# A new order of steps for a gated attention with an MLP behind it, on one core

## The chip, the core and the metric

One core of a Trainium2 chip runs the whole kernel as one program. The metric is the device time of an execution in microseconds (us). The engines are named as in the profile: PE (TensorE), DVE (VectorE), ACT (ScalarE), POOL (GpSimd) and SP (SyncE, which issues all DMAs here). Each engine runs its instructions in the order in which the program lists them; between engines, semaphores keep the data right.

## The reference, cut to what matters

```
# gateloop: B, H, S, D = 4, 8, 768, 48
mag = sqrt(a_re*a_re + a_im*a_im)
scale = minimum(mag, 0.999) / (mag + 1e-6)
a_re_n, a_im_n = a_re*scale, a_im*scale
for t in range(S):
    new_re = ar*S_re - ai*S_im        # ar, ai: row t of a_re_n, a_im_n
    new_im = ar*S_im + ai*S_re
    kv = outer(k[t], v[t])            # for each batch and head
    S_re, S_im = new_re + kv, new_im
    y[t] = q[t] @ S_re
# act_prelu: 3072 tokens, d_model 384, d_ff 2048
x = y.transpose(0, 2, 1, 3).reshape(B*S, H*D)
h = x @ w_in
g = maximum(h, 0) + alpha * minimum(h, 0)
out = g @ w_out
```

All of it is float32. A state of 48 x 48 complex numbers runs through 768 tokens for each of 32 heads, with a complex gate for each token and row; its outputs are the tokens of a two-layer MLP with a PReLU.

## The kernel before, in words

The scan over tokens is done in chunks of 128 tokens: 4 batches of 6 chunks make 24 units, each for all 8 heads. Within a unit the gate's magnitude and phase are applied by a tree of levels 1, 2, 4, 8, 16 and 32.

The work is written as 39 generators, the tasks. Each `yield` ends a step, and a step issues one instruction or a few. A task's letter is its place in the list.

- **Gates, letters A to I** (`gates`, from line 223). Gate A makes the decays and phases of the first chunk of batch 0, B those of chunks 1 and 2, C those of 3 to 5; D to I take three chunks of a batch each. The large steps are DVE's (the products L338, the sums L340, the last products L426 and L429) and ACT's (the functions L257 to L281, the copies L366 and L368 that turn a pair of re and im into three). In gates with 3 chunks, the small products of the phase scan are cut: the level of 128x72 (L338) and its sum of 128x36 (L340) run on GpSimd for the late gates, seven of each, then come ACT's copies L366 and L368, a second short chain on GpSimd (128x12 and 128x6), again L366 and L368, and further steps with L391, L396, L405, L407 and L413. The results go to DRAM (decs, phs).
- **Loads, letters J (q, k, phases PP and decays T of each unit), K (half rows of v, copied from DRAM to DRAM, L560), L (v in several row orders, L603 to L629), M (the raw weights, L491)**, and **n** (the MLP's input xT, L873).
- **Weights, letters N and O.** Each weight piece comes as 64-bit words and is made into float32 by three ACT steps (L507, L509, L511), one on GpSimd (L515, 128x768) and two on DVE (L517, L519).
- **Units, letters P to Z and a to m** (`unit`, from line 645). A unit turns keys and queries by the phase (DVE, L661 and L663), multiplies them up the levels (DVE, L717, six times), has copies of half of them made (ACT, L740 and L756), multiplies keys with queries on PE (L678) and masks the results (L699 on ACT, L702 on DVE). Then come transposes (PE, L785), the state's update (PE L797, DVE L826 and L829), the outputs (PE L817 and L841), their copy from PSUM (ACT, L855) and a DMA to DRAM (ysc).
- **The MLP, letter o** (`all_mlp`, line 926). The 24 units' tokens make 14 groups: two of one unit, ten of two units, two of one. For each group and each of 16 blocks of 128 features: three matmuls (L889) into ps_h, ACT's Relu (L896), DVE's scaled sum (L898). With a block of lag come the output matmuls (L908) into ps_o; after 16 blocks ACT copies ps_o out (L918) and SP sends it (L921). ps_h has two buffers, ps_o one.

Buffers come from pools: three KQ, one PP, two T, one V and one VL, two xT, three states St, two ps_lv, one tile for each of ps_misc and ps_y.

What sets the order of all work is one string, ORDER (from line 30), with one letter for each step: `Plan.run` (L96) goes through the string and advances the task of each letter by one step. The numbers that the steps yield (estimated durations and what they wait for) are not used when the kernel is built. So an engine's queue is exactly the order in which the string reaches its instructions, and a buffer is reused in the order in which the string reaches its tiles. The string has 4292 letters. GpSimd is told from DVE in the gates by the size of the step (`small`, `on`), not by the string.

```
    def run(self, order):
        for c in order:
            next(self.tasks[self.LETTERS.index(c)], None)
```

Of the kernel before, what the change touches and what calls it, by code (L numbers as in the profile page):

```python
# [27 lines left out]


ORDER = (  # L30
    "AABAMMAAAAAAAAAAAAAAAAAMAAAAAMABJMNAJNNABNAAAAAAAAAAAAANKJKAKBKNBAABAAAABABBJAAAALAAAAAAABAMAAAAOKAK"
# [4 lines left out]
    "ooCRCNCRLRMKOCCOCDONCJDQQMNDQCODNCRDCDRCCQNQOLCQCROCOMLRCLRMOCLODoDQJCLCCRQKRCCQCooLooLCLRQDLLLLLLCN"
    "QoRCDRDCDCoCKCCRCRCCCoRRRDoCKRRooRQCRCoCoooCJQQQRQooDRNoDoRRRQDJCRDRoNooooJooJoooRJoDoooORDooooooLLL"
    "LLLoooDODoDnoRDooRoOoERDRooNNRRLDoRoSRRoooNOoNooSoEooOoooNOSLOoSoNROSSoooSJDooSJJSJSLSJOooooooSSSooS"
    "SLSoDooELoLLSSooooooDSSLESoJSJoSSSSSooDooSSToDoooSDoSoETDEDTDoJoSSoSSJJSSEDoTSoooKJoTTooKooLDDoEoDoS"
    "LTKTToToDoDLSoLoDoTKoEEDTDSSoTTToSDDDLDoJLSoSSSooooSoDoDDEoooDToTToooDoEoLoooLDTnooDUoDLooEooooooEDo"  # L40
    "oEToTTDDDDDToToDJJJETJUooDoTDToooUoTTLLLEooLooooLToDUDETUTUUToETTTToUoDLDDoUDUDoUDTDoooooUooKDoKTLUo"
    "EUTUTTTEDDDLDoEEEoDoooooJJoDoTTKKoTToooELoooEDoooooTLUUDUULoLooLooLLoooooDoUDEUooEoETEoDooDoooooEooo"
    "LooLUUUUoEUUEoUEoLEEoooooUEUoEoUooEEooEUoooJoVUUUUJJUoJUEUVUUEoUUUUEEVJEEEFVoVooVoJoooooVVVoJUVUoooV"
    "oJFEoVVoJonoJooVWooVooWVVFoEFVLoooLoVEoLLLLLLVoooWLooooVoLWEEEEEEEEEEEEEEEoLooLoLoLKWoWVFJVEEVWJVVVo"
    "VooWooVVVoooVoWoVoKWWVoVJVVWoVVWWJEVVFEEEEEVEEJEEEWWVoLWooWoLoLLLLLEWLoEEXoFEKoLooEoWWWEFWXVWWFLWVEo"
    "LLVFLLooWVoooVVVVFJJJJEJoooWoooWEooWEWooWWWWEWEEWWEWWWEooWEWoLEXLWFoWFLoooLoXoLWoWoLoLoEoFooXXFXooFX"
    "oooooFELWLoLJXLJLoKoXXooLooFoooFoXoooooXXXFFXoooXXoXoooFFooFFXXoXLXXYooXFXFooXWJFXoXJooXnoXXYoYoooXX"
    "XooJJJoYFoFXFFoGXFXXFJLXXFYYFXFFXYXLXLXooGoLLLFXoooXooLJXooYoYLYFFoJJoooYoooGFoKYoFoFoooJYFFFYYZFGFo"
    "ZFFoFoYooJooYoYoooYooGooZoZFYYYYFYoFFFFYFJFJFFLoFooLoYoooYoJoLYYLooGoYLZLZYoooYoGYYYYFYFLZFLLZZGYFYY"
    "LFoYFZYYGYFLZFFFFFFZGFFFFFFaoYYoFoYoooooYYLLoZZZoLZoZnoLoZoooooooJFFLoLLLLZGJJJoJFoZFFFFZoKZGoZZFaFZ"  # L50
    "FooooooZZFZoKZoooFFooFooooZZooZZZZZZFZJZoZZGGZoZoZFooaZZZZooaGGaLoZGLoaaGJooLoooaaoLLLLaLJooJaJoLoaG"
    "ooooooLooooooaaooGabaooGooboooooaoGaboaLoHGHoGboooobGooboooGaaabaaaaGaabooKKGJoGaLLbbKoaoooaGGbboGoo"
    "GaoaaaaJaGaGoaKGaaHHaGaGaJGoGGGGoaGoJoaooaoKKooHoHHLooGcGoGoJbbGoGoocHoooooooLbboLLLGGGboJJJJobcoLoo"
    "oGooLoLGLocbbobooGGoooooocbcLLLbbbbbcnoboboHbGJcboobcoocooLLbbooobbcHGGbbbcbHoGoGGGGcLcGcGbGHLLLLobH"
    "HbGJHLLLGocobboobGLGGcGGGoccboooboooGoLGLGooHGoocccoGHocLdbdbbcocGoccGoJcGGooLLoocooHcGoHooGGoJKcGoJ"
    "JGGGGGGGHoooooocodcccccoHLLLLoLLoooLdooLoccGGGoHdoodooodLHdoIdoooooodJodoIoooooooLLLHHcocooooodLHooo"
    "oHooddccdooododHHdcodoJIoHHcHdddddddddHHHcoocoooKJccoHLooooooooodoooeJdHooJooondooddHHdHdHdJedoJdIdo"
    "dJddIddddoHooeoHodoJdHoooLedJJJeIeeeHeHoHooLeHoooLHIeooooooHJHeoooeLILeLHoLoLeooLIoLeeJfefofKooofHeo"
    "oooooLoooLoefefeofLeoooeIJeIILoeeooeoeHHHeHHHoHHHHHHHofeoJoIeoeeefeoefeeeIIefeeIJeooeoooIofeeooIeooo"
    "eoLLfffIfooHooooJofffIoIoooJLgJoggHLJHHHHHooooLLooooKHLoLoHoJLoLKLKLLLHgHHfggooIHHfooonffffoffHoooJf"  # L60
    "foHHofooKHHfoKfggHggoooIIIIoHooHoffffHfffffffHooLLHLHHLoLoooooHoHoIogHoooHoooIoIofHgooooooIoofIoIfLo"
    "HIIfLLLLLggggKoIoooooogJgooooIfoKgoooooLoggfgoLoohggIhggoooghogoIgoooJggoIohJooIJgggggggggJKgIIggJJI"
    "ghooIhLggoohohoLoogLJLohhoJhhooohhooooJooohhhioohIIoJoihoooIIooIihooiohnoooooooLIIILLohihihLhoohhhJo"
    "IhhoooLoohiJLLoLoLIIoiIIhIIIohIhILIioooIhhhhhhhhhLhJhoohIIIiiiIJIooLIIIoIhIIIIhhoojLhLooohooooooiiio"
    "iojLiooooJiJioJLLLojoIjoLoooLLLLLoooooooiIiIJIiijiIjiiiIooooIiiIoiooIjioIoooooIojIIIooIooooJioiiIjii"
    "ijoiiLiiLiLILiiiojoijooiIioLjiLjJIjILIoLoLojoooJoJjoooojoooooooJoooojoojjJojoojJoLooLoooookLoooojLko"
    "ookLojjjjokojoJkknJoJoookoojoookjoooojoooojjkkjjlojjokLkkkkjLLLLLLLLjLokooooookoookkoooooojokkkkkkkj"
    "okjjjjjoooLLooooLLooookkoooooooooooooojoookooookokokkkkkkkkokkkjJloooooooooooooooookJoolookookolooll"
    "llolLoookooolJloJJoJkoolLoJoomlkllolnooooooooloooooooJJmlooLooooolmooooooomooolmolmooollolllLLoooooL"
    "moLoLLooloomolmlLLmLLoolooooloLlmooooooooooolllllmmLoommmLooooooooooooooooooooLoooooooommooooomLoomm"  # L70
# [930 lines left out]
```

## Time and profile before

| what | value |
|---|---|
| median of 3 runs | 836.58 us (833.38 to 837.02) |
| profiled execution | 836.36 us |
| its span in the trace | 834.6 us |
| mean granted TensorE clock | 0.962 |
| PE busy | 695.8 us, 83% of the span |
| DVE busy | 651.7 us, 78% |
| ACT busy | 438.7 us, 53% |
| GpSimd busy | 200.6 us, 24% |
| DMA | 130.91 MB, 157 GB/s on average |

The span runs from the first to the last instruction in the trace; the execution's own time is 1.8 us longer. Busy time counts compute instructions only. In the rows of instructions, a name such as "ps_h<-xT,w_in_sb" gives the output and the inputs, then the shape (partitions x elements), then how often. A wait is written as the engine that idles, the line that it then runs, and what released it.

### The profile page before, as it was taken

Reading aid. Unit: us, or ns where it says so; the run is one execution under the profiler, and the core shown is the slowest. Engines: PE = TensorE matmul, PEld = TensorE weight load, DVE = VectorE, ACT = ScalarE, POOL = GpSimd, SP = SyncE. Lnnn points to the kernel's source line nnn. Section 1 sums busy time; section 2 is a strip of 40 time slices with the busy share of each in tenths; the row PEclk is TensorE's granted clock in tenths of the full one; section 3 lists DMA queues with packets and bytes.
Section 4 is the critical chain, followed back from the end, with each engine's and each line's share of the span. In section 5 each row is a group of like instructions: output and inputs, shape, how many; then the busy total and the mean of one; then the engine's idle time right before and its main releaser. Section 6 shows DMA issues by size and latency. Waiting matters only on the chain.

```text
span 834.6 us, 26848 instructions
## 1 busy us (share of the span) xinstructions
PE 695.8 (83%) x11488; PEld 527.7 (63%) x11488; DVE 651.7 (78%) x1020; ACT 438.7 (53%) x937; POOL 200.6 (24%) x293
## 2 busy tenths in 40 slices
PE   0001435889998999899999999999999999999998
PEld 0001424667776777677777777777777777777776
DVE  5989999999997899889988988979767652644112
ACT  7758787467635665565657446644344342323221
POOL 5231222328603600360135103330341000000000
PEclk9999755899999999999999999999999999999999
DMA  6696977786478579737873586457834832511110
GB/s 195 189 280 157 274 170 227 217 220 175 100 222 209 145 171 248 186 88 197 233 194 77 158 259 159 115 143 216 210 99 118 202 70 61 136 34 43 35 30 10
DMA packets 194174, 130.91 MB, mean 157 GB/s; under 512 B 74120, under 2 KB 185864, under 8 KB 194056
## 3 DMA queue, kind: packets, MB, share of 16 engines
q1 hardware_dynamic: 194056, 129.20, 58.8%
q8 instruction: 90, 1.47, 0.7%
q14 instruction: 28, 0.23, 0.1%
HBM read 100.82 MB, written 35.71 MB: 164 GB/s over the span
## 4 chain that ended last, share of the span: by engine, by line
PE 53%; DVE 23%; DMA 12%; POOL 4%; issue 4%; ACT 4%; SPq 1%; DVEq 0%; ACTq 0%; POOLq 0%
PE ps_o L908 22%; PE ps_h L889 20%; DVE KQ L717 4%; DMA T<-decs 4%; PE ps_lv L678 4%; DVE gate L426 3%; DVE gate L338 2%; PE ps_y L817 2%; DMA phs<-gate 2%; PE ps_y L841 2%; PE ps_kv L797 2%; DVE gate L429 2%; DMA g_sb<-in_w_out_dram 1%; POOL gate L338 1%; DVE gate L340 1%
## 5 line engine op out<-in xcount | busy, mean ns | idle before, releaser
L889 PE MATMUL ps_h<-xT,w_in_sb 128*128 128x256 f32 (+1 forms) x1344 | 297.3, 355 | 9.0 <-DMA xT<-ysc 7.0
L908 PE MATMUL ps_o<-w_out_sb,g_sb 128*128 128x384 f32 x768 | 297.2, 500 | 7.9 <-DVE g_sb L898 4.5
L889 PEld LDWEIGHTS ps_h<-xT,w_in_sb 128*128 128x128 f32 x1344 | 235.7, 194 | 82.1 <-DMA xT<-ysc 7.8
L898 DVE SCALAR_TENSOR_TENSOR g_sb<-g_sb,al,ps_h 128x256 f32<-128x256 f32 (+1 forms) x224 | 97.5, 436 | 117.9 <-ACT g_sb L896 117.6
L896 ACT ACTIVATE g_sb<-ps_h 128x256 f32<-128x256 f32 (+1 forms) x224 | 78.8, 352 | 200.7 <-PE ps_h L889 199.4
L908 PEld LDWEIGHTS ps_o<-w_out_sb,g_sb 128*128 128x128 f32 x768 | 136.5, 191 | 59.4 <-DVE g_sb L898 7.0
L717 DVE TENSOR_TENSOR KQ<-KQ,T 96x1024 f32<-96x1024 f32 x120 | 149.2, 1246 | 23.8 <-PE ps_lv L678 15.2
L678 PE MATMUL ps_lv<-WQ 96*32 96x32 f32 x2304 | 34.3, 204 | 72.6 <-DVE WQ L661 56.2
L678 PEld LDWEIGHTS ps_lv<-WQ 96*32 96x32 f32 x2304 | 26.5, 116 | 92.7 <-DVE WQ L661 56.2
L740 ACT COPY WQ<-KQ 96x1024 f32<-96x1024 f32 x48 | 49.9, 1040 | 22.2 <-DVE KQ L717 22.2
L338 POOL TENSOR_TENSOR gate<-gate 128x72 f32<-128x72 f32 x42 | 25.8, 615 | 134.3 <-ACT gate L368 131.5
L515 POOL TENSOR_SCALAR top<-top 128x768 f32<-128x768 f32 x16 | 41.2, 2578 | 65.2 <-ACT top L507 65.1
L756 ACT COPY W<-KQ 96x512 f32<-96x512 f32 x48 | 30.9, 644 | 40.1 <-DVE KQ L717 30.3
L338 DVE TENSOR_TENSOR gate<-gate 128x576 f32<-128x576 f32 (+5 forms) x84 | 48.6, 579 | 3.8 <-ACT gate L368 2.4
L855 ACT COPY T<-ps_y 48x256 f32<-48x256 f32 x96 | 31.6, 365 | 34.5 <-PE ps_y L841 33.7
L817 PE MATMUL ps_y<-A,VL 64*48 64x64 f32 x2304 | 42.0, 224 | 4.4 <-issue 3.8
L426 DVE TENSOR_TENSOR gate<-gate 128x1152 f32<-128x1152 f32 (+2 forms) x36 | 43.6, 1235 | 0.1
L817 PEld LDWEIGHTS ps_y<-A,VL 64*48 64x48 f32 x2304 | 39.7, 125 | 5.4 <-issue 4.5
L699 ACT ACTIVATE A<-ps_lv,columns 128x64 f32<-128x64 f32 x144 | 37.6, 334 | 9.2 <-PE ps_lv L678 9.1
L678 PE MATMUL ps_lv<-KQ,W 96*32 96x32 f32 x1536 | 24.5, 203 | 20.3 <-ACT W L756 19.7
L702 DVE TENSOR_TENSOR A<-ps_lv,mask 128x256 f32<-128x256 f32 x96 | 37.6, 412 | 0.0
L717 DVE TENSOR_TENSOR KQ<-WQ,T 96x1024 f32<-96x1024 f32 x24 | 29.5, 1231 | 6.4 <-DMA T<-decs 4.2
(106 smaller groups left out, 899.4 us busy)
## 6 DMA issues: line engine op xcount, KB each, us to landing
T<-decs SPq DMA_DIRECT2D x48, 384.0 KB
PP<-phs SPq DMA_DIRECT2D x24, 387.0 KB
KQ<-in_q_dram SPq DMA_DIRECT2D x48, 192.0 KB
decs<-gate SPq DMA_DIRECT2D x7, 1152.0 KB
phs<-gate SPq DMA_DIRECT2D x14, 576.0 KB
KQ<-in_k_dram SPq DMA_DIRECT2D x40, 192.0 KB
vsc<-in_v_dram SPq DMA_DIRECT2D x48, 144.0 KB
VL<-vsc SPq DMA_DIRECT2D x24, 288.0 KB
```

Of the source, the lines that this page charges most:

```text
L338: on(4 * k).tensor_tensor(out=m, in0=w[:, 1::-1].unsqueeze(2).to_broadcast([P, 2, 2, k]), in1=pairs_of(u), op=ALU.mult)
L426: TT(out=m[:, a], in0=U5[:, 1 + a], in1=turned(off3, o)[:, a].unsqueeze(1).unsqueeze(3).to_broadcast([P, L // 2, nb, 2]), op=ALU.mult)
L515: nc.gpsimd.tensor_scalar(out=top, in0=top, scalar1=F64_SMALL, scalar2=None, op0=ALU.max)
L678: nc.tensor.matmul(t[64 * i + j:64 * i + j + HC // 2, p], lhsT=keys(n, g), rhs=queries(n, g), start=True, stop=True)
L699: nc.scalar.activation(a[:, :, cols], t[:, :, at:at + name], AF.Copy, scale=s)
L717: nc.vector.tensor_tensor(out=x, in0=x if x0 is None else x0, in1=m, op=ALU.mult)
L740: nc.scalar.copy(z.rearrange("p i n t -> p i (n t)").rearrange("p i (m h) -> p m i h", h=h), bass.AP(tensor=KQ.tensor, offset=KQ.offset + ...
L817: nc.tensor.matmul(o, lhsT=Vp[h][64 * i:64 * i + 64, s, e_ * D:(e_ + 1) * D], rhs=a, start=False, stop=False)
L889: nc.tensor.matmul(p, lhsT=w_in_sb[:, f // 2, kk, f % 2 * P:(f % 2 + 1) * P], rhs=x_of[m][:, kk], start=(kk == 0), stop=(kk == NK - 1))
L896: nc.scalar.activation(gt, p, AF.Relu, scale=-1.0)
L898: nc.vector.scalar_tensor_tensor(out=gt, in0=gt, scalar=al_1[:, f:f + 1], in1=p, op0=ALU.mult, op1=ALU.add)
L908: nc.tensor.matmul(sums[0], lhsT=gt[:, c * P:(c + 1) * P], rhs=w_out_sb[:, f], start=(f == 0), stop=(f == NF - 1))
```

## The change

The string ORDER is another one. Nothing else differs: the same 4292 letters, each as often as before, the same functions, buffers and instructions on each engine. Since the order inside a task is fixed, only the way in which the tasks are woven into each other differs. The new string was chosen by a search that counts the holds of GpSimd and VectorE on each other and the length of the DMA queue. Of the diff, which replaces all 43 lines, the first two lines and the last two:

```diff
 ORDER = (
-    "AABAMMAAAAAAAAAAAAAAAAAMAAAAAMABJMNAJNNABNAAAAAAAAAAAAANKJKAKBKNBAABAAAABABBJAAAALAAAAAAABAMAAAAOKAK"
-    "AOBAAABMAAABAAABBBABLLBABAOMABAKBABABBBALNBNABABAABBOBAKBNBABBNOBNBOOOABBBOBMBBBNLONNBBBBBBOBLBBBOBN"
...
-    "ooooooooooooooooooooomoooooooooooooooomooommmmmmmmmmmmmoooooooooooommnoooooooooooooooooooooooooooooo"
-    "oooooooooooooooooooooooooooooooooooooooooooooooooooooooooooooooooooooooooooooooooooooooooooo"
+    "AAABAAAAAMAAAAAAAAAAAAAAAAAMMMBAAAAMJNAAAAAAAANJNNAAABANANAABBAABAJAKJABAAMAAAABBAAAAAABAOAAOAAKABAA"
+    "LMAAABAAABABBBLBALBABOAOMBAABLBBBNABAABABNAABABBNBABALABLOBOMBNBBKKONOBOBBNBBBJLBOBJBOBLBNBBBJBBBBBB"
...
+    "oooooooooooooooooooooooooooommmmmmmmmmmmmmmoooooooooooooooooooonoooooooooooooooooooooooooooooooooooo"
+    "oooooooooooooooooooooooooooooooooooooooooooooooooooooooooooooooooooooooooooooooooooooooooooo"
 )
```

Placed instruction by instruction, the two orders differ as follows (work of the same engine that stands ahead of it, each piece at its duration in the trace of before). The mean shift is 1.3 us on PE, 1.4 on DVE, 1.2 on ACT and 0.2 on GpSimd. Larger moves are these:

- Ahead of the first feature matmuls of the first group stand 100.7 us of DVE work, before 90.3; ahead of the second group's 166.9 in both.
- The half-row copies K stand eight places earlier among SP's DMAs, on average; the weight loads M stand a few places later, the one of 126.27 us two places.
- In the head, unit 2's copy L740 and gate C's second L368 stand behind the ACT step L507 of the weight piece that this load feeds.
- ACT's steps of gates G, H and I (L366, L368 and the steps behind them) stand earlier by up to 21 us of ACT's time. The memset of gate I (L305) stands behind gate H's first chain on GpSimd, where it stood within the gate's chains.

More of the change, by code (lines that the diff above doesn't have):

```diff
@@ L30 @@
 ORDER = (
-    "AABAMMAAAAAAAAAAAAAAAAAMAAAAAMABJMNAJNNABNAAAAAAAAAAAAANKJKAKBKNBAABAAAABABBJAAAALAAAAAAABAMAAAAOKAK"
-    "AOBAAABMAAABAAABBBABLLBABAOMABAKBABABBBALNBNABABAABBOBAKBNBABBNOBNBOOOABBBOBMBBBNLONNBBBBBBOBLBBBOBN"
-    "NOBBJBKJBNJBPBBBBBOBPBBPBBBPBCCBBOBKBPPPBNLBMPJCKBBCPLBLKKPBMBBOPKKOKBBCBPBCBPMBCBPBLPBNCLPLCPLBPBCP"
-    "CLPCCCNPJJJCJONJNPCDCPPPPPPPPPPDPCPPCJMPCCPKPCPCQCQCNOCDPJCNCQCNLQCCPQJJCPCPQCDQPPNOPOCOQCOPJPCQPPPC"
-    "DOQMCQNCQDLJQJnCQLQJCQCKKKLQDDQKOLCCKoQCKNONCQLLNCRCQNQCRQCQRNQDQQKCQMQODLCLRDQCRLNRRDDCLLORCQOLCQON"
@@ L36 @@
[L36 to L70, printed above, removed]
@@ L71 @@
-    "lllllomLlLlllooloooooooooLLLoomlooLlnommooooooooooommLomooomooooooooooooooooooooooooLLmooooooooooooo"
-    "ooooooooooooooooooooomoooooooooooooooomooommmmmmmmmmmmmoooooooooooommnoooooooooooooooooooooooooooooo"
+    "AAABAAAAAMAAAAAAAAAAAAAAAAAMMMBAAAAMJNAAAAAAAANJNNAAABANANAABBAABAJAKJABAAMAAAABBAAAAAABAOAAOAAKABAA"
+    "LMAAABAAABABBBLBALBABOAOMBAABLBBBNABAABABNAABABBNBABALABLOBOMBNBBKKONOBOBBNBBBJLBOBJBOBLBNBBBJBBBBBB"
+    "NBBNBBBKOBBPBPBPBBBBOPOLBNPBBCJBPCLOMBBCMNBKKBPKKKKBBPPBPMKCBPBBBOKOBCPBBBPPCBLBBJPPLPBNPKCCJCBCPCCC"
@@ new lines @@
+    "JNNPCPCPBPCOLCPPPPPPPKNPCKPKNLJCPPJJPCDNPPKCPJCCCNDCPPOJKKCQPCNNPCPPOLJLNOCLCCMOMQCPQQCOQCQQCQCQCDPL"
+    "PDQPPPQCDDQQQCLQPNJCCOCQCOQCQCCQCNDCJLRCQQKQCCLnNJCRJLCDDDQQOCORNCCQNQQLOOQQCLKCOKCKRDCoDJNLDRNQCCNC"
+    "MDLJLLCNCRMQDQCORQCQQORMCNKRCRoNODDCDOCNRQRCOQCOCCCCCQKOCMJQOLLoCRQLORCDCLLRKoDRQDLLLCCQNooooCQRRLCR"
+    "QQDQCCoDJLLDoCCoCDCMoooRoDQoRCQLLLoRoDRRDCCCoooRoQDDCCRRDoNRRODRNRoooRRDooDnRRoRRoooooDOoLLJoRNOoJDo"
+    "oooJDLooooRooLNooNoDRooOJRODROSSooRNoLooooooOooSooENooRSooRSoSJSNoRSERRLRSoSSooooOJLLSJLoooDoSooESJL"
@@ new lines @@
+    "LSoSSOoSSoJoLoooooEoLSLDSSDooooSoSSSTSJoSSDoooTSSSooDEToooDSESSSJDoSSooToooSooETJTSJLTLooTTDLoDDDDDE"
+    "KSoooJToESSDoDTDoEToLoSKSoSDDoKSTTToooDoDoooJooDKEDSSoooDTTTDoLooTooLooooEooToEEJoEooUoTooUDEoooDooT"
+    "DoDDoLTooJTLLLLLLTDooULooooTETTooTooDToEoDUDDDDDDDDTUoUooTTUoEooUnoUKDUDUKKoooToJJJDJEoETTTTLLLoUoDU"
+    "DULEEoELoTUooTLKDoUDoELLoKDoTDDooDoDDDoooDEDTToEooLLoEooDoooUoooooTToTooDUooLDoEoTEoUooDooooUUEoooTo"
+    "EoEoUoLUUooUUTEoUEEooULEoooUooUoEUKoJJEooEoooUEUJoJUUUUUoVUEUVJUUVFVVEooEUUUVooooooJoVJVEUUoEVFoEVEE"
@@ new lines @@
+    "JooVnVJoJooLVooooooFoWooooWVoVoFFVEEEELLLLLLVLLLooVVWooVooooooEVEEoEooWooWooVVVWoLLWWWEEEEEELEEVVVVV"
+    "ooEoVooVLooFVWVEooVVJVJFJVJKVWEFVVWWWEoVJEEEEEVooWFLXLLLEEWEEooWooLoLooooLWEVVWEVEWEKWXEVVVVWLLLLWLo"
+    "WFoooEWEEEELEoWoVVooWWEEooooLWEFFWooooooWoEJFoJoWooWWWJEEEEWoWWLoXLoLoEFFooooWoWooooJLLWXXXWFWWWoLXL"
+    "ooLoXXWWLoJXWFooWoooXoJooFXoooFXXoXoXooXXJooXoLooFoooFoXXXXLoLYLXXoXLXJoonoXXoXoXooXJXoJJFGFYXFoXoYY"
+    "FoFooGGoXXXFFXFKoKFKYFXYFFYFXFFooFFJYoLoooooLYoXoYXXXoJoFooLoFYFJFFGoLLLLoooooXoXXXYYoYoYYoYooYJJFoY"
@@ new lines @@
+    "oooooJooZoYYFFYYoZYGYoYoFoLFooooZoLoZooooJoFZZYLZYFoYoFFooJYFFFFFFFFFFFFFFFYoYLLLLoKGZGYYYYYJYZYKJoY"
+    "YLLZYYGoLZGoooKoLoZYYKooLFFFGLZLLLGZYYFYZYZoFoFFFFFFFFoFKZZoZFFooFooaoFoFoooaooZGoZFLLLZLLFJZoFZFZJZ"
+    "FZooZoFooZZGFFFoFFoonoooFooooGZoZooZaZFZoJZZoJooGoZZoJooZZaoooaaaGaZZZoZZJZLGJZZoaooLLLGoooooaGaoJoo"
+    "oLbooKooJooooLGooabGaGbaoaGaoooGoaaoooooaoGoooLLGLooboobooboaabababaGaooaJoLLaaLoaoaooaaoGJLJGGGGoGo"
+    "HGaaaHaaaoGJaaoabGGGGJbGLbGLaaLGHoLaaLooLaobcHGoaoooJJbooJoooGooHGbbooLGoHoobbobobcoooGGHbooGcoooooo"
@@ new lines @@
+    "oGGGGGGoHooooobbcbHbccbLLcGLLobHLbLooboGKGboGGGGobooobocbbLGcHcoocGoKbcGGJGGGGbbbHbbbKGbcbJGJccGGGcn"
+    "LooJLLLGLGLLLcHLLLLLcHooLcoooGobbbcGcbbGGbbccooobGGooGooodoJJooocoHcGcHHGoocodooooooKGoooccJGGHoGooo"
+    "oGooGcooococHGoJoHooGcccGdccoJcGcLGooodHHHLoHLooooJKoooLHddodHoHodododGodoooLLoooIcooodIoocdodHLdodc"
+    "HcdLcoHdooccLLHLdIJoHHHcHooHoooocoLoodIdoddoKoodocddddoooeooddooLooodoHHooHooHKHoooLoodHoHodJdHHHHoH"
+    "HHIJJdddddJedHoHndddHHdJJLdHeooJooLedodooeddeeoeoLooLHeeeIooHoooooHHHHHHHHHHooHKeoeJJeLoIIeooooofoLo"
@@ new lines @@
+    "LeLLLfeLLoooooeefIfooooooooeefeeeooefefoeeoHHHHHeeofIHoooHLLoeHfIooHHHooHeHeeeeIHeeeeeefJeHfoHJIoHeL"
+    "oefHoJIoHLoJIffoffeJeIIeeLoofoJoooofHLLooofoogIoooffJfoofffoHofofofLooJLLLogofooJKLIofooHLoHogooongo"
+    "HLLfoLgKHgHgooooooooooooofogogJIfgfffffIgIfffHLJIIoogfIIfILHKoHofHfooLLooooooggLgffgoooooogooooggoIo"
+    "ooIHffgILIgogIgIogoLoILIoggooIgoJoLoooLoooILILIIoooogogooghIoLgohoggghhgJogJgggJggooKJgJJggIoIooghhJ"
+    "gIIIIohoohgoooohoooooIIIIihIJIoIIIoIJoIooioIoohoJLhhJoooooooooLohLhIihIIIIIhiLoLLLLLLLLLLoonohoooooo"
@@ new lines @@
+    "hhoooohiohoihoohIIIIIoooihhhiohoJhJohiIhiioohooooIIIIIIIIIohoohhhhhhioooooooohhohooiohihhIIIooooiihh"
+    "IiohhiooooooLoihohiJiiiLJLJLoLLLooooiLLLjLiooIIoiiJjooIojjIIioIIooooooooLojjjLIooooooiooioJoLoijoioo"
+    "iiIijJiiijJLoIjiiiiiiiiiioIoooooooIiIoLoooInjLLoojjooooooLjjoooojoooJoojjoooJJooLjjjjjjjkkojooojoooo"
+    "oooLkoLokLjoooojookkkkkoLLjooLLoLkookojokojjjjjkoJkkokLLokoooojjkJJJoooLooLoooookjookjkkjkokLjkoojoo"
+    "kjojkoLokkooLoooooLooooLoooLoooojJolLLkjlLoookkoLokkkjkJkJkkkkkkoookooJlJoooooooookoLookolkJLklJJoko"
@@ L73 @@
+    "loooooloooonJooooJomoloolololoooooooooooooLoooooollllomolomloloooooloooooooooooLommlmLlLLooloooooooo"
+    "ooooollolloommmmoLoloollooooooolmloLLLLLLoomlommmmllolllooolmommololmlmmlomlllloommLLLLLLmooLooooooo"
+    "oomooolollooooooooooooooooooooooooooLooooooommmLLoLonooooooooooomLLmoooooooooooooooooooooooooooooooo"
+    "oooooooooooooooooooooooooooommmmmmmmmmmmmmmoooooooooooooooooooonoooooooooooooooooooooooooooooooooooo"
     "oooooooooooooooooooooooooooooooooooooooooooooooooooooooooooooooooooooooooooooooooooooooooooo")
```

## The prediction

> **What bounds the kernel now.** The page comes first, with the slices of PE and DVE (busy tenths, 40 slices).
>
> ```profile
> PE   0001435889998999899999999999999999999998
> ...
> DVE  5989999999997899889988988979767652644112
> ```
>
> A slice is 20.9 us. PE is full only from the ninth slice on, and DVE is full from the second to about the twelfth. So the kernel has a head, in which VectorE sets the pace, and a body, in which TensorE does. The view of busy time by stretches puts numbers on both. Its columns are us; PE, PEld, DVE, ACT and POOL busy (and instructions); granted clock, DMA share, GB/s.
>
> ```profile
> 0.00:60.00 60.00, 0.66 (x32) 0.52 (x32) 46.59 (x138) 39.34 (x62) 24.60 (x38) 1.00 0.79 218
> 60.00:100.00 40.00, 12.47 (x428) 10.70 (x428) 39.79 (x55) 33.05 (x47) 7.43 (x4) 0.95 0.80 216
> 100.00:160.00 60.00, 30.61 (x742) 25.21 (x743) 58.17 (x101) 42.88 (x74) 17.15 (x9) 0.58 0.73 198
> 160.00:184.00 24.00, 19.68 (x306) 15.15 (x305) 23.92 (x42) 15.12 (x29) 6.37 (x4) 0.93 0.94 253
> 184.00:400.00 216.00, 203.40 (x3675) 154.37 (x3674) 196.44 (x268) 124.56 (x281) 77.24 (x119) 0.99 0.68 174
> 400.00:560.00 160.00, 159.25 (x2732) 119.60 (x2731) 141.72 (x197) 94.53 (x202) 48.20 (x84) 1.00 0.65 169
> 560.00:834.60 274.60, 269.74 (x3580) 202.13 (x3578) 145.08 (x225) 89.27 (x246) 19.64 (x35) 1.00 0.37 97
> ```
>
> At 184 us the second group of feature matmuls starts (L889). Up to there DVE is busy 46.59 + 39.79 + 58.17 + 23.92 = 168.5 us, so it idles 15.5, most of it in the first stretch; PE is busy 63.4 of the 184. After 184 PE is busy 632.4 of 650.6 us. The span is then the time at which the head lets PE go (184), plus 632 us of matmuls that no order can shorten, plus what PE still idles, 18.2 us. What the change could win in the body is a part of these 18; what it could win in the head is DVE's idle time and whatever lengthens DVE's instructions. PE's own list of waits, from 184 us on, says what the 18 are made of (us in total, times, longest).
>
> ```profile
> PE ps_o L908 <- issue: 3.0, 1, 3.0
> PE ps_y L841 <- DVE St L829: 2.2, 2, 1.5
> PE ps_h L889 <- DMA xT<-ysc: 2.1, 1, 2.1
> PE ps_lv L678 <- ACT W L756: 1.8, 5, 0.6
> PE ps_h L889 <- issue: 1.3, 1, 1.3
> PE ps_o L908 <- DVE g_sb L898: 1.0, 1, 1.0
> PE ps_y L817 <- issue: 0.9, 1, 0.9
> PE ps_lv L678 <- issue: 0.8, 2, 0.5
> ```
>
> With three smaller rows this makes 14.1 us; the rest is the tail after the last matmul. The "issue" rows, 6.0 us, name no wait, and I leave them where they are. About 8 us remain that an order can touch.
>
> **The change part by part.** The diff shows only letters, so I counted: for every instruction, how much work of its own engine stands ahead of it in each order, each piece at its duration in this trace. The instructions are the same ones, and inside a task their order is the same. An instruction moves by 1.3 us on PE, 1.4 on DVE, 1.2 on ACT and 0.2 on GpSimd, as a mean over the engine. PE's work ahead of the second feature group is 64.0 us in both orders, and DVE's is 166.9 in both. The large shape of the schedule therefore stays: the 184 us and the 632 us are the same sum as before, and what is left are local terms.
>
> *Term 1, DVE's stalls in the head.* DVE's waits in the first 200 us:
>
> ```profile
> DVE gate L259 <- ACT gate L257: 5.3, 1, 5.3
> DVE gate L338 <- ACT gate L368: 2.4, 1, 2.4
> DVE gate L269 <- ACT gate L267: 2.3, 1, 2.3
> DVE gate L396 <- ACT runs L368: 1.7, 1, 1.7
> ```
>
> The first and third lie in the opening of gate A, where both orders have one thing to do; they stay. The second (gate B's first product, at 49.7 us) has more DVE work in front of it in the new order than the ACT copy needs, and I expect it to go: **−2.4 us**, all on the path, since DVE is the bound there.
>
> *Term 2, the weight piece in the head.* The fourth wait is that of gate C's product (L396, at 142.3 us) for ACT's copy. The new order puts two ACT instructions, unit 2's copy L740 and the gate's L368, behind the ACT instruction that opens a weight piece (L507), and that one waits for its load, which the new order issues two DMAs later on SP:
>
> ```profile
> 126.27 5.01 DMA g_sb<-in_w_in_dram
> 131.37 0.90 ACT L507 ACTIVATE top<-g_sb 128x768 f32<-128x768 f32 x1 [0.85 <-DMA g_sb<-in_w_in_dram]
> ```
>
> ACT waits 0.85 us for it now. The load takes 5.01 us, so the gap that ACT hands on to DVE lies between nothing (1.7 us better than now) and the whole load (3.3 worse). I take 3.0 us, near the upper end because ACT already waits here: **+1.3 us**. The copies of half rows (L560) come eight places earlier on SP and a weight load moves behind them; the load is due only some 5 us after it would land, so I cost it at nothing, and if that cover is gone it too costs up to the 5.01 us of one load.
>
> *Term 3, holds between DVE and GpSimd.* How long the engines keep each other is seen in the spread of one form's durations (ns, minimum/median/maximum), here for DVE's decay product, GpSimd's small gate sums and its weight step:
>
> ```profile
> L717 DVE TENSOR_TENSOR KQ<-KQ,T x120: 1206/1216/1818, 62.5 to 763.1; 96x1024 f32<-96x1024 f32 x120
> ...
> L340 POOL TENSOR_TENSOR gate<-gate x42: 258/262/1328, 192.4 to 607.2; 128x36 f32<-128x36 f32 x42
> ...
> L515 POOL TENSOR_SCALAR top<-top x16: 2118/2348/4090, 15.6 to 169.2; 128x768 f32<-128x768 f32 x16
> ```
>
> ```profile
> L717 DVE TENSOR_TENSOR KQ<-KQ,T 96x1024 f32<-96x1024 f32 x120 | 149.2, 1246 | 23.8 <-PE ps_lv L678 15.2
> L340 POOL TENSOR_TENSOR gate<-gate 128x36 f32<-128x36 f32 x42 | 25.5, 607 | 3.2
> ```
>
> GpSimd pays most: L340 loses 607 − 262 = 345 ns a time, 42 times, 14.5 us. DVE pays little: L717 loses 30 ns a time, 3.6 us in 149.2, or 2.4%. At that share the holds of the whole head cost DVE 4 us (2.4% of 168.5); counted form by form against each form's short durations I find about 8. So the most that a better placing can give on the path is −8, and the same instructions placed worse cost about +2. GpSimd's order hardly changes, so I take a small part: **−1 us**. In the body the holds lie on engines that have spare time.
>
> The Trainium skill ("SBUF — State Buffer", section "Who interferes with whom") speaks of an exclusive lock: a DVE operation with two SBUF inputs and a GpSimd operation that reads SBUF keep each other out for the whole instruction. GpSimd's 258 to 1328 ns agree with that; DVE's 1818 ns at most, 0.6 above its median, do not show a wait for a whole L515 of 2.3 us. By the rule in full, each of the 16 L515 could hold DVE up to 2.3 us, 38 us in all, against the 8 that the rows bear out; the sum goes by the rows.
>
> *Term 4, PE's short waits in the body.* Set against the DVE work that each matmul needs, the new order gives PE more room between 300 and 420 us (the 1.5 us wait for L829 is inside) and less between 420 and 600 (by count, four places at which the operand would come 1.7 to 3.6 us late, where it is in time now). If all waits that can go went, −8; if each of the late places cost its part, +8. PE has two ps_h buffers of features to work on meanwhile, so I take **−0.5 us**.
>
> *GpSimd and ACT in the late gates.* In gates G, H and I the small products run on GpSimd and hand over to ACT copies (L366, L368). Now ACT comes to them late, and GpSimd waits for ACT:
>
> ```profile
> POOL gate L338 <- ACT gate L368: 131.5, 6, 39.3
> ...
> POOL gate L338 <- ACT runs L368: 32.4, 6, 9.7
> ```
>
> The new order puts several of these ACT steps 10 to 20 us earlier, so that they stand within 3 us of GpSimd's end (G's L366 2.6 us ahead of it by count, I's 3.2). Where ACT comes first it must wait, in order, with the Relus (L896) and the copies W (L756) behind it. I cost it at nothing because two ps_h buffers, about 3 us of matmuls, cover it, and keep it as the main rival. Gate H's end on DVE stays (514.2 us of DVE work ahead instead of 515.0).
>
> **Sum.** −2.4 + 1.3 − 1 − 0.5 = −2.6 us. The profiled execution took 836.36 us (1.8 outside its span of 834.6) and stands 0.2 under the median of 836.58, so no correction is due: 836.4 − 2.6 = **833.8 us**. A difference of about 0.5%, 4.2 us, is what a measurement of this kernel can tell from no change; 833.8 lies inside it.
>
> **The rivals.**
>
> *Slower: ACT waits for GpSimd in gates G, H and I.* Place: L366 of these gates. Price: GpSimd's first chain in gate H, of its timeline (start us, us, instruction) the first two rows and the last:
>
> ```profile
> 507.83 0.44 POOL L338 TENSOR_TENSOR gate<-gate 128x72 f32<-128x72 f32 x1 [24.24 <-ACT gate L368]
> 508.35 1.13 POOL L340 TENSOR_TENSOR gate<-gate 128x36 f32<-128x36 f32 x1
> ...
> 515.34 1.33 POOL L340 TENSOR_TENSOR gate<-gate 128x36 f32<-128x36 f32 x1
> ```
>
> Its fourteen products and sums take 8.8 us, 507.8 to 516.7, with four of the sums held to over 1.1 us. If ACT stands before it with 3 us of its work still to do, and then once more at the short second chain, the gate costs about 3 us of PE beyond the two buffers, three gates 4 to 10 us: 840 to 846, say **843**. It decides once the ACT step stands more than 3 us ahead of GpSimd's end, and by count two stand at 2.6 and 3.2. Against it: GpSimd too can be faster if its holds go, and the profile has PE waiting for ACT only 1.8 us in all.
>
> *Slower by the head.* The new order feeds the first feature group later (10.4 us more DVE work stands before its first matmul). The granted clock in the head is low:
>
> ```profile
> 100.00:120.00 20.00, 4.70 (x174) 3.72 (x178) 20.00 (x31) 15.61 (x23) 5.50 (x2) 0.50 0.79 181
> 120.00:140.00 20.00, 11.73 (x294) 10.20 (x296) 19.87 (x42) 16.19 (x22) 5.74 (x3) 0.50 0.86 262
> ```
>
> If PE works thinner around 140 us and the clock stays at 0.50 some 20 us longer, up to half of PE's 14 to 19 us there is added: 836.4 + 8 = **844**. With term 2 at its worst (+3.3, and a second load late by 5) the head gives the same.
>
> *Faster: holds and body waits both go.* −8 in the head, −2.4, and −4 of the body's 8: 836.4 − 14 = **822**; half of that, 829, is the likelier figure.
>
> *Nothing.* The average instruction moves by little over 1 us. If the waits only change places, the time is **836.4**, within 1.
>
> **How the numbers follow.** Forecast, 831 to 836: 0.34. Nothing: 0.12. Faster (822 to 831): 0.24. Slower by ACT and GpSimd: 0.20, by the head: 0.10. Under 832.4 lie the faster rival and a quarter of the forecast: 0.30. Over 840.8 lie nearly all of the two slower ones: 0.29. Between them: 0.41. The range leaves out the end of the faster rival and the end of the slower ones: 825 to 847.
>
> **What would show it.** Right: the DVE gap at 49.7 us gone; a DVE gap of about 3 us near 142 behind L507; L717's mean near 1240 ns; the first feature matmul of the second group at 182 to 184 us; PE's waits from there on 12 to 15 us in all. Wrong: PE waiting for L896, W or g_sb near 445, 520 or 600 us with ACT's row naming POOL as its releaser; clock 0.50 past 160 us; or a DVE busy sum up to 184 us more than 4 us below 168.

## The result, and the profile after

| kernel | median us (range, runs) | traced execution | span |
|---|---|---|---|
| before | 836.83 (833.38 to 842.39, 20) | 836.36 | 834.6 |
| after | 833.65 (828.86 to 838.60, 20) | 831.98 | 830.2 |

The ratio after to before is 0.9957, with a 95% interval of 0.9938 to 0.9975: 3.6 us faster by this ratio (the medians lie 3.2 us apart), inside the range and 0.15 us from the forecast of 833.8. That the number is right does not make its terms right, and the experiments show that most of them were not. One thing to keep in view: executions of one kernel spread over 9 to 10 us, and a trace is one execution.

The slices of PE, DVE and of the granted clock, after:

```profile
PE   0001515789999999989999999999999999999998
...
DVE  5999999999998899889998988999658644552112
...
PEclk9999997899999999999999999999999999999999
```

The shape is that of before: a head with DVE full, a body with PE full. What differs at sight is the clock, which fell to 0.7 and 0.8 in two slices, where before has 0.7, 0.5, 0.5 and 0.8 in four. That is this execution and not the order: a second trace of after (e10 below) has 0.7, 0.5 and 0.5. The stretches, with the same columns and borders as for before:

```profile
0.00:60.00 60.00, 1.29 (x64) 1.04 (x64) 48.61 (x140) 40.33 (x63) 24.12 (x38) 1.00 0.77 221
60.00:100.00 40.00, 12.64 (x400) 10.75 (x396) 39.10 (x54) 33.22 (x46) 7.62 (x4) 1.00 0.80 206
100.00:160.00 60.00, 28.77 (x740) 23.30 (x741) 58.92 (x102) 42.12 (x74) 21.72 (x9) 0.89 0.75 217
160.00:184.00 24.00, 18.86 (x309) 14.56 (x308) 23.15 (x39) 15.44 (x30) 6.98 (x6) 1.00 0.81 201
184.00:400.00 216.00, 207.17 (x3692) 156.98 (x3691) 199.96 (x274) 129.20 (x285) 83.56 (x118) 1.00 0.70 181
```

Up to 184 us DVE is busy 169.8 us (before 168.5) and so idles 14.2 (before 15.5). It ran the same number of instructions by then, 333, and the second feature group starts at 184.1 us, before at 184.2. The head gave nothing. From 184 to 400 us PE is busy 207.2 us of 216, before 203.4. So the gain of this pair of traces lies behind the head. PE's waits there, after (us in total, times, longest):

```profile
PE ps_y L817 <- issue: 2.6, 2, 1.6
PE ps_y L841 <- issue: 1.6, 1, 1.6
PE ps_kv L797 <- ACT T L788: 1.5, 1, 1.5
PE ps_o L908 <- DVE g_sb L898: 1.4, 2, 1.2
PE ps_h L889 <- issue: 1.2, 1, 1.2
PE ps_kt L785 <- DVE KQ L717: 1.2, 1, 1.2
PE ps_o L908 <- issue: 0.7, 1, 0.7
```

Of before's list the xT wait (2.1) and the wait for St L829 (2.2) are gone, and of the wait for W L756 (1.8) 0.4 is left; the named waits fell from 8.1 to 4.9 us, the "issue" ones rose from 6.0 to 6.8. DVE's waits in the first 200 us, after:

```profile
DVE gate L259 <- ACT gate L257: 5.3, 1, 5.3
DVE gate L269 <- ACT gate L267: 2.4, 1, 2.4
DVE g_sb L898 <- ACT g_sb L896: 1.0, 2, 0.8
DVE columns L213 <- PEq L990: 0.9, 1, 0.9
DVE gate L338 <- ACT runs L368: 0.5, 1, 0.5
DVE gate L407 <- ACT gate L405: 0.5, 1, 0.5
DVE gate L338 <- ACT gate L368: 0.3, 1, 0.3
```

Both gaps of the terms 1 and 2 (2.4 and 1.7 us) are gone, and yet the head is not shorter. The durations, after, of DVE's decay product, GpSimd's small sums and its weight step (ns, minimum/median/maximum):

```profile
L717 DVE TENSOR_TENSOR KQ<-KQ,T x120: 1205/1218/1428, 60.2 to 747.4; 96x1024 f32<-96x1024 f32 x120
...
L340 POOL TENSOR_TENSOR gate<-gate x42: 259/263/2580, 191.8 to 589.8; 128x36 f32<-128x36 f32 x42
...
L515 POOL TENSOR_SCALAR top<-top x16: 2136/2383/6511, 15.6 to 167.5; 128x768 f32<-128x768 f32 x16
```

L717 is held less (at most 1428 ns, before 1818), and GpSimd seems to be held more (L515 up to 6511 ns, before 4090; L340 up to 2580, before 1328; GpSimd's busy time rose from 200.6 to 215.3 us). Second traces of both kernels (e4 and e10 below) repeat this for L717 (at most 1807 before, 1429 after) and for L340 (1318 and 2579), but not for L515, which reaches 6934 ns before and 6516 after; GpSimd is busy 210.1 and 217.3 us there. DVE's sum up to 184 us did not fall in either pair.

### The profile page after: what moved, and what is told of

Its sections match the earlier page's. It is cut to its first block, busy times and chain, and to the rows that moved or that the text cites. A ratio compares the mean times of both kernels' runs of the same rounds, so it can differ in the third digit from the quotient of the medians.

```text
span 830.2 us, 26838 instructions
## 1 busy us (share of the span) xinstructions
PE 692.1 (83%) x11488; PEld 525.0 (63%) x11488; DVE 650.5 (78%) x1020; ACT 441.5 (53%) x937; POOL 215.3 (26%) x293
## 4 chain that ended last, share of the span: by engine, by line
PE 68%; DVE 14%; ACT 4%; POOL 4%; DMA 4%; issue 3%; SPq 2%; DVEq 0%; ACTq 0%; POOLq 0%
PE ps_o L908 27%; PE ps_h L889 26%; PE ps_lv L678 4%; PE ps_y L817 4%; DVE KQ L717 3%; PE ps_kv L797 3%; PE ps_y L841 2%; PE ps_kt L785 2%; DVE gate L338 2%; DMA T<-decs 1%; POOL gate L338 1%; POOL gate L340 1%; DVE gate L340 1%; DVE gate L298 1%; DVE gate L426 1%
## 5 line engine op out<-in xcount | busy, mean ns | idle before, releaser
L908 PE MATMUL ps_o<-w_out_sb,g_sb 128*128 128x384 f32 x768 | 294.4, 497 | 9.9 <-DVE g_sb L898 9.0
L889 PE MATMUL ps_h<-xT,w_in_sb 128*128 128x256 f32 (+1 forms) x1344 | 296.3, 353 | 1.2 <-issue 1.2
L889 PEld LDWEIGHTS ps_h<-xT,w_in_sb 128*128 128x128 f32 x1344 | 232.8, 191 | 71.3 <-issue 2.0
L908 PEld LDWEIGHTS ps_o<-w_out_sb,g_sb 128*128 128x128 f32 x768 | 136.1, 190 | 61.2 <-DVE g_sb L898 11.6
L717 DVE TENSOR_TENSOR KQ<-KQ,T 96x1024 f32<-96x1024 f32 x120 | 146.8, 1226 | 27.5 <-PE ps_lv L678 24.2
L678 PE MATMUL ps_lv<-WQ 96*32 96x32 f32 x2304 | 34.4, 204 | 77.5 <-DVE WQ L661 54.2
L678 PEld LDWEIGHTS ps_lv<-WQ 96*32 96x32 f32 x2304 | 26.4, 116 | 97.1 <-DVE WQ L661 54.2
L515 POOL TENSOR_SCALAR top<-top 128x768 f32<-128x768 f32 x16 | 44.8, 2802 | 82.3 <-ACT top L507 70.6
L740 ACT COPY WQ<-KQ 96x1024 f32<-96x1024 f32 x48 | 50.0, 1041 | 10.9 <-DVE KQ L717 10.8
L756 ACT COPY W<-KQ 96x512 f32<-96x512 f32 x48 | 30.8, 641 | 31.2 <-DVE KQ L717 23.5
L817 PE MATMUL ps_y<-A,VL 64*48 64x64 f32 x2304 | 42.7, 224 | 3.9 <-issue 3.9
L817 PEld LDWEIGHTS ps_y<-A,VL 64*48 64x48 f32 x2304 | 40.2, 126 | 5.6 <-issue 5.3
L678 PE MATMUL ps_lv<-KQ,W 96*32 96x32 f32 x1536 | 24.9, 204 | 18.4 <-ACT W L756 18.2
L785 PE MATMUL ps_kt<-ident,KQ 96*128 96x96 f32 x192 | 25.7, 258 | 14.3 <-DVE KQ L717 9.3
```

What stands on the lines that cost most here:

```text
L515: nc.gpsimd.tensor_scalar(out=top, in0=top, scalar1=F64_SMALL, scalar2=None, op0=ALU.max)
L678: nc.tensor.matmul(t[64 * i + j:64 * i + j + HC // 2, p], lhsT=keys(n, g), rhs=queries(n, g), start=True, stop=True)
L717: nc.vector.tensor_tensor(out=x, in0=x if x0 is None else x0, in1=m, op=ALU.mult)
L740: nc.scalar.copy(z.rearrange("p i n t -> p i (n t)").rearrange("p i (m h) -> p m i h", h=h), bass.AP(tensor=KQ.tensor, offset=KQ.offset + ...
L785: nc.tensor.transpose(t[:, p], KQ[:, 1, 4 * i + p], ident[:D2, :D2])
L817: nc.tensor.matmul(o, lhsT=Vp[h][64 * i:64 * i + 64, s, e_ * D:(e_ + 1) * D], rhs=a, start=False, stop=False)
```

## The experiments

All ran on chips on which the kernel before took 840.6 to 841.3 us; each ratio is to the kernel before, run on the same chip, and it is not quite the quotient of the medians. The times that the first four expectations name stand on the 836.4 us of the first trace, so they too are to be read as ratios. A place in the string tracks time: place 850 is at 187 us, 1200 at 240 and 1400 at 275, and up to place 850 or 1200 the two orders have placed the same steps but for two and one. So orders can be joined there; "then old" means the steps not placed yet, in the old order.

**First theory (M).** Lining the two traces up by the work that PE has done, the new order is level with the old one at 215 us and 5 us ahead at 275. In between, PE waits for xT of group 3 (groups are counted from 0, so the one that starts at 184 us is group 1) in the old trace and then shows a granted clock of 0.50 for 3.4 us. So the load's place was to be the cause.

```diff
-ORDER = old
+ORDER = new up to 1200, then old
```

> The new order up to 240 us, the old one behind it. Theory M (the gain is made between 240 and 275 us, where the old order has PE wait 2.1 us for xT of group 3 and then run at half clock for some 3 us; in the head gains and losses cancel): 835.5 to 838 us, group 1's features start at 184 us, and PE waits for xT of group 3 again, 1 to 3 us. Theory H (the gain is made in the head, as the prediction's terms 1 to 3 have it, and only shows later): 832.5 to 834.5 us.

Measured: 837.57 us median, ratio 0.9948 (0.9927 to 0.9970). Theory M's 835.5 to 838 us are 0.999 to 1.002 of 836.4, so it falls, although 837.57 as a time lies inside: the whole gain is there without the new order's middle. PE's wait for xT was 0.2 us, not 1 to 3.

```diff
-ORDER = old
+ORDER = old up to 1200, then new up to 1400, then old
```

> The old order, with the new one from 240 to 275 us only. Theory M: 831.5 to 834 us, PE does not wait for xT of group 3, and from 275 us on each piece of work is 3 to 5 us earlier than in the old order. Theory H: 836 to 838 us.

Measured: 840.74 us, ratio 0.9999 (0.9977 to 1.0022). PE waited for xT no more, and nothing was won.

```diff
-oooVVVoJUVUoooVoJFEoVVoJonoJooVWooV
+oooVVVoJUVUnoooVoJFEoVVoJooJooVWooV
```

> The old order with one letter moved: group 3's load of xT is issued right behind unit 5's two stores, ahead of a load of PP, one of a gate's a_im and one of T. Theory M, narrowed to that load: 832.5 to 834.5 us, no wait of PE for xT of group 3. Rival (the loads behind it are as urgent, or the new order's middle stretch gains by more than this load): 836 to 839 us, with DVE waiting for PP or T instead.

Measured: 843.26 us, ratio 1.0027 (1.0009 to 1.0045). The xT wait is gone, and the kernel is slower. DVE does not pay for it at PP or T, as the rival had it: it waits 0.9 us for PP between 186 and 340 us, against 1.2 in the first trace of before.

> The kernel before once more, for its trace. Theory M: PE waits 1 to 3 us for xT of group 3 again, with a granted clock under 1 behind it. Rival (that wait was an accident of one execution): no such wait, and the time is the same 836 us.

Measured: 840.20 us in the one execution. PE's waits from 186 us on, in the kernel before, second trace:

```profile
PE ps_y L817 <- issue: 4.5, 2, 3.0
PE ps_y L841 <- DVE St L829: 2.6, 2, 1.5
PE ps_o L908 <- issue: 2.4, 1, 2.4
PE ps_lv L678 <- issue: 1.9, 2, 1.1
PE ps_lv L678 <- ACT W L756: 1.6, 5, 0.5
PE ps_h L889 <- DMA xT<-ysc: 0.9, 1, 0.9
```

The xT wait is 0.9 us here, not 2.1, and one L817 waits 3.0 us with no name where the first trace had nothing. The place at which the first pair of traces drew apart was in good part the luck of two executions. Theory M was read from a difference of two single traces, and that is what failed.

**Which stretch?** Theory B puts the gain into 187 to 240 us, theory H into the head.

```diff
-ORDER = old
+ORDER = new up to 850, then old                        (e5)
+ORDER = old up to 850, then new up to 1200, then old   (e6)
+ORDER = old, its letters J, K, L and M up to 1200 at their places in new   (e7)
```

> The new order up to 187 us only, the old one behind it. What the traces so far have in common: between 186 and 300 us PE idles 6.9 to 12.4 us in the kernels with the old order ahead of 240 us, and 1.6 to 1.7 in those with the new one. Theory B (the start of the body, 187 to 240 us, makes the gain, through the matmuls and loads woven there): within 0.3% of before, and PE idles 6 us or more in 186 to 300. Theory H (the head makes it): 0.4 to 0.6% faster, under 3 us of idle.

> The old order, with the new one from 187 to 240 us only. Theory B: 0.4 to 0.6% faster than before, PE idles under 3 us between 186 and 300 us, with no late instruction packet in unit 4's L817 at 217 us and none at 283 or 296 us. Theory H: within 0.3%, 6 us or more of idle.

> The old order, in which up to 240 us only the loads (letters J, K, L and M) stand where the new order has them; all compute steps and xT's loads stand as before. Theory L (the loads moved ahead take traffic out of 240 to 300 us, where PE's instruction packets and xT come late): 0.4 to 0.6% faster, PE idles under 3 us between 186 and 300 us. Theory W (it is the weave of the compute steps): within 0.3%, or slower where a load now holds another up, and 6 us or more of idle.

```diff
-ORDER = new
+ORDER = new up to 850, then old up to 1200, then new   (e8)
-ORDER = old
+ORDER = old up to 850, then new                        (e9)
```

> The new order, with the old one from 187 to 240 us only. Theory B (that stretch makes the gain): within 0.25% of before, 0.4 to 0.6% slower than the new order whole, and PE's waits from 186 to 305 us sum to 7 us or more. Rival (the gain is spread over the order): 0.2 to 0.4% faster than before, with waits of 4 to 6 us.

> The old order up to 187 us, the new one behind it. Theory B, with a head that gives nothing: as fast as the new order whole or up to 0.3% faster, 0.4 to 0.8% faster than before, PE's waits from 186 to 305 us at most 5 us. Rival (the new head feeds the body better): within 0.25% of before.

> The new order whole, once more. Theory B: 0.4 to 0.5% faster than before, PE's waits from 186 to 305 us 3 to 5 us, of them no xT, and at most 2.5 us that are neither xT nor issue. Rival (the two traces differed by chance): waits of 7 us or more, as in the old order.

The idle times from which the first of these expectations starts (6.9 to 12.4 and 1.6 to 1.7 us) are not what the waits of the profile give: from 186 to 300 us they sum to 7.1 to 9.2 us in the four traces with the old order and to 3.6 and 4.8 in the two with the new one. The difference is smaller, but it is there.

What was measured, with PE's waits between 186 and 305 us from each kernel's trace ("issue" and named, summed):

| new order in | median us | ratio (95%) | waits 186 to 305 us: issue + named |
|---|---|---|---|
| nothing (two traces) | 840.6 to 841.3 | 1 | 2.5 + 4.8; 6.2 + 2.6 |
| head (e5) | 842.86 | 1.0025 (0.9991 to 1.0058) | 5.3 + 5.5 |
| loads up to 240 (e7) | 843.44 | 1.0009 (0.9979 to 1.0038) | 5.1 + 5.1 |
| 187 to 240 (e6) | 840.12 | 0.9973 (0.9938 to 1.0007) | 4.4 + 2.1 |
| up to 240 (e1) | 837.57 | 0.9948 (0.9927 to 0.9970) | 2.6 + 2.2 |
| all but 187 to 240 (e8) | 841.83 | 1.0001 (0.9971 to 1.0032) | 2.8 + 4.5 |
| all but the head (e9) | 835.43 | 0.9917 (0.9892 to 0.9943) | 1.4 + 5.7 |
| all (e10; the result's trace) | 837.05 | 0.9942 (0.9915 to 0.9969) | 2.9 + 3.0; 1.4 + 2.2 |

Theory B holds in its main point: where 187 to 240 us is old, nothing is won (e5, e7, e8), and where it is new the mean is below 1 each time, though e6's interval still touches 1 and its medians alone would give 0.9992. Three pieces (head, 187 to 240, the rest) that add up, fitted with equal weight to seven ratios (the table's but e7's, and the result's 0.9957), come out at +0.18%, −0.51% and −0.21%, or about +1.5, −4.3 and −1.8 us, and miss none of them by more than its interval. The traces agree on the place. The first feature matmul of group 4 has as many matmuls ahead of it in each of these orders (3992 in the trace). From group 1's first to it, 144.4 and 145.6 us pass in the two traces of before, 139.9 and 141.7 in those of after; with the old stretch it is 142.6 to 152.1 us (five traces), with the new one 139.9 to 143.0 (five). From there to the end of the span before takes 506.0 and 508.2 us, after 506.2 and 511.8: nothing is won behind about 330 us.

What makes the gain in that stretch is less clear. With the old order there the waits from 186 to 305 us sum to 7.3 to 10.8 us, with the new one to 3.6 to 7.1, on average 8.9 and 5.6 (e2 and e3, which change what follows that stretch, have 7.1 and 13.0). Of these 3.3 us, 1.8 are "issue" waits and 1.5 named ones. But the traced executions are not typical: e6's and e8's are the fastest of their kernels (836.14 and 836.80 us), e5's and e9's the longest of theirs (848.25 and 836.95), and e8 and e9, 0.8% apart by their ratios, show 7.3 and 7.1 us of waits. So the waits are weaker evidence than the ratios.

Three expectations missed: e6 was named 0.4 to 0.6% faster and came to 0.27, with waits of 6.5 us instead of under 3, one of them an "issue" wait of 3.0 us at 298 us where none was expected; e9's waits were 7.1, not 5, although it is the fastest; e10 came to 0.58% instead of 0.4 to 0.5, with waits of 5.9 us instead of 3 to 5 and named ones of 3.0 instead of at most 2.5. Moving the loads J, K, L and M alone (e7) does not make the gain. Which of the compute steps between 187 and 240 us does was not taken apart further.

**What are the "issue" waits?** They differ by 3.4 us between two traces of the kernel before. In the first one, the longest is at 336.61 us; the row of PE's timeline, and the queue row of the DMA view of the stretch 333.6 to 335.2 us (packets, MB, share):

```profile
336.61 0.81 PE L908 MATMUL ps_o<-w_out_sb,g_sb 128*128 128x384 f32 x2 [2.97 <-issue]
```

```profile
q8 instruction: 1, 0.02, 5.4%
```

A packet of 16384 bytes of the queue named instruction ran in that stretch, from 333.77 to 335.15 us in the trace, while PE stood still, and PE went on 1.46 us after its end. This is so each time: of the 63 issue waits of seven traces (before twice, after twice, e9, e11 and e12), all 63 end 1.2 to 1.7 us behind the end of such a packet. The next two experiments move the packets' borders. To the kernel before are added small matmuls into a PSUM tile that nothing reads, at the start, when PE has nothing to do; a matmul takes two PE instructions, a weight load and the product, and the trace counts 64 more of each.

```diff
+    pad = ps.tile([P, 2, 512], F32, tag="y", name="ps_y")
+    for _ in range(64):      # e12: range(128)
+        nc.tensor.matmul(pad[0:D, 0, 0:P], lhsT=nothing[0:64], rhs=ident.bitcast(BF16)[0:64, 0:P], start=True, stop=True)
```

> The old order, with 64 small matmuls (128 instructions of PE) at the very start, into a PSUM tile that nothing reads, while PE has nothing else to do. Theory C (PE's waits named issue are waits for its own code, which comes in packets of 16384 bytes, and so sit at fixed counts of instructions): the issue waits at L889 near 284 us, at unit 6's L817 near 297 and at L908 near 334 are gone from there and turn up about 128 instructions away, at other lines; the time stays within 0.4%. Rival (they belong to these instructions): they stay at L889, L817 and L908 at the same pieces of work.

Measured: 874.54 us, ratio 1.0395 (1.0367 to 1.0423), 33 us slower where at most 0.4% was expected. PE's issue waits from 60 us on in that kernel, of its list of waits (its lines stand four further down, so L845 is L841, L821 L817, L682 L678):

```profile
PE ps_y L845 <- issue: 11.1, 7, 2.6
PE ps_lv L682 <- issue: 10.0, 6, 3.0
PE ps_y L821 <- issue: 9.9, 6, 2.2
...
PE ps_h L893 <- issue: 2.1, 2, 1.1
```

From 186 us on there are 19 issue waits with 30.3 us, against 5 with 6.0 in the first trace of before (6 with 9.4 in the second); the named ones stay (7.0 and 8.1). They left their places, as the theory had it; that there would be three to four times as many was not foreseen. The stalls are not all of the loss: PE's busy time behind 184 us is 645.2 us, against 632.4 in the first trace of before. In this trace each of the six stalls of over 2 us goes with 3.4 or 6.8 us at a granted clock of 0.50, 27 us in all, against 3.4 us behind 186 us in the first trace of before. Is it the position, or the added instructions themselves?

> The old order with 128 small matmuls at the very start, which are 256 instructions of PE, the size of one code packet (16384 bytes), instead of 64 (half a packet). Theory C, by position (what counts is where the borders of the packets fall in the later work): the borders fall as in the kernel before, so the time is within 0.6% of before and PE's waits behind a code packet, from 186 us on, sum to 7 to 12 us as there. Rival (the added instructions or their work at the start cost the 33 us that half a packet did): 3% slower or more, with 25 us or more of such waits.

Measured: 841.82 us, ratio 1.0022 (0.9998 to 1.0046). With twice as much added, the 33 us are gone: it is the position that counts, as theory C has it, and 256 instructions shift the borders by one whole packet. Its waits from 186 us on:

```profile
PE ps_y L821 <- issue: 6.7, 3, 3.8
...
PE ps_o L912 <- issue: 3.5, 1, 3.5
...
PE ps_lv L682 <- issue: 1.4, 2, 0.9
PE ps_h L893 <- issue: 1.3, 1, 1.3
```

They sum to 12.9 us, a little above the 7 to 12 expected (the traced execution, 849.4 us, was the longest of this kernel's twelve), and the long ones stand where theory C has them in the kernel before: L889 at 286 us (1.3), L817 at 303 (3.8), L908 at 346 (3.5).

This leaves a rival open for the gain itself. A new order also moves the work at which PE's packet borders fall, and more than half of the waits that the new stretch saves on average are "issue" waits. The kernel after was not run with its code shifted, so what the weave saves by operands that come sooner and what by packets that fall better is not separated.

## Why the prediction was right, and where not

The forecast was −2.6 us for a measured −3.6 (interval about −5 to −2). Its parts were head −2.1, body −0.5. The runs show about nothing or a small loss in the head, and the whole gain in the body, so the sum came out right by luck: its terms make up for each other. One chance was added up wrong as well: by the prediction's own terms the one under 832.4 us is 0.24 plus a quarter of 0.34, or 0.33, not 0.30.

- **"The large shape stays."** Right: the second feature group starts at 184.1 instead of 184.2 us, and PE is busy 630.5 us behind 184 in place of 632.4.
- **Term 1, the gap at 49.7 us (−2.4, "all on the path").** The gap went, the time did not come: e5, which has the new head alone, is 0.25% slower in the mean (its interval includes 1), and e9, which lacks it, is the fastest. The step that failed is "all on the path". DVE's idle time up to 184 us fell by only 1.3 us (1.5 in the second pair of traces), since shorter waits appeared elsewhere, and its busy time rose by as much.
- **Term 2, the weight piece (+1.3).** Wrong in size and sign: the gap at 142 us is gone in both traces of after. ACT's L507 did not wait for a load between 124 and 140 us in the first.
- **Term 3, holds (−1).** In the head wrong in sign in this trace: DVE's busy sum up to 184 us rose from 168.5 to 169.8; in the two second traces it is 168.0 and 169.5. The 2.4% were read from L717 over the whole span and laid on the head, but its 20 instructions up to 184 us had a mean of 1214 ns before, below the median of 1216, and 1217 after: what L717 wins lies behind 184 us (1252 to 1228). That its mean over all falls to near 1240 ns was right in direction (1226). That GpSimd is held, up to 6511 ns or nearly three times its L515 median, agrees with the exclusive lock that the Trainium skill describes ("SBUF — State Buffer", "Who interferes with whom"). That one instruction keeps the other engine out for its whole length does not show: five of DVE's sums and products ran during these 6.51 us, and no L717 waited for a whole L515 here either.
- **Term 4, PE's waits in the body (−0.5).** Waits for St, W and xT were named as what could go, but the size was not: the body gives about −6 us by the fit, of it −4 in the stretch 187 to 240. I had said that the room gets better between 300 and 420 us and worse from 420 to 600; the hybrids put most of the gain ahead of that. The named waits, for which the sum allowed 8.1 − 0.5 = 7.6 us, are 8.1 and 6.1 us in the two traces of before and 4.9 and 5.9 in those of after; all waits behind 186 us are 14.1 and 15.5 before, 11.7 and 16.9 after. So the fall of the first pair is not repeated by the second, whose executions (840.20 and 839.74 us) differ by less than the medians do.
- **"The issue rows name no wait, and I leave them where they are."** This was the real gap. They are waits for PE's code: 6.0 and 9.4 us in two traces of one and the same kernel, 6.8 and 11.0 in after, and a shift by half a packet makes them 30.
- **Rival ACT and GpSimd in the late gates.** It did not happen in G, H and I, where PE has no wait for ACT. It shows once, in gate F. ACT's timeline and PE's, after:

```profile
354.91 0.22 ACT L366 COPY runs<-gate 128x36 f32<-128x36 f32 x1 [2.82 <-POOL gate L340]
355.04 0.21 ACT L368 ACTIVATE runs<-gate 128x18 f32<-128x18 f32 x1
355.16 0.46 ACT L787 COPY T<-ps_kt 128x384 f32<-128x384 f32 x1
355.52 0.27 ACT L788 COPY T<-ps_kt 128x128 f32<-128x128 f32 x1
```

```profile
355.84 0.85 PE L797 MATMUL ps_kv<-V,T 64*64 64x48 f32 x39 [1.46 <-ACT T L788]
```

  ACT waits 2.82 us for GpSimd, unit 9's copies stand behind it, and PE pays 1.46 us. The mechanism exists; its price here is 1.5 us (1.7 in the second trace of after), not 4 to 10.
- **Rival of the head's clock.** It did not happen: between 160 and 184 us the granted clock is 1.00 in both traces of after and 0.93 in both of before. Nor does a low clock in the head show in the time: of the 20 executions of after, 6 have a mean granted clock of about 0.99 and 14 one of 0.96 to 0.97, with medians of 833.8 and 833.7 us. That DVE is the bound there would explain it.

The version with the old head and the new order from 187 us on (e9) beats the kernel before, with 0.9917; beside the whole new order on the same chip it is 1.6 us faster (835.4 and 837.1), which the intervals do not separate.

## What to carry to other kernels

A stall that disappears from the engine that sets the pace is not yet time won: ask what that engine does next, and check the time at which the following stage starts. Do not explain a change of half a per cent from one pair of traces; take a second trace of the same kernel and join the two versions at a few points, and let the ratios say which stretch matters. Where PE's waits are named "issue", look for the packets of the instruction queue, and try the same kernel with PE's code shifted by half a packet before you credit or blame an order.

## What the runs showed of the hardware that was not expected

PE's code arrives in packets of 16384 bytes, 90 of them in the kernel before. Of the 78 that come from 186 us on, PE stood still behind 4 to 10, for 6 to 13 us in all, except with the shift by half a packet, which made it 19 and 30 us and the kernel 33 us slower; a whole packet of shift undid that. The restart came 1.2 to 1.7 us behind the packet's end in all 63 waits of the seven traces. The Trainium skill ("Runtime: NRT & Kernel Launch", section "Instruction fetch mechanics") gives blocks of 16 KiB, or 256 instructions, and calls the crossing of a border mostly hidden. The size agrees with the traces, the 256 with the experiment. Mostly hidden holds by count here, at 68 or more of 78 borders; the others cost this kernel about 1% of its time, and 4% more with an unlucky shift. Why a packet comes late at some borders and not at others stays open: neither the traffic nor the mix of short matmuls around a border was varied alone.
